# Attention before two expert layers: the masks of the scores, the 1e-9 of the softmax, the warm-up and the table of places

## The chip, the cores and the metric

The kernel runs on one core of a Trainium2 chip. The metric is the device time of one execution in microseconds, as the median of several runs. One execution was also recorded by the profiler; all rows of a trace are from that one.

## What is computed

```python
def reference(**kw):
    x = attention(kw["q"], kw["k"], kw["v"])        # each (2, 12, 448, 64)
    x = x.transpose(0, 2, 1, 3).reshape(896, 768)
    x = moe(x, w_gate, w_val, w_out)                # 768 -> 1536 -> 768
    return moe2(x, w_in, w2_out)                    # 768 -> 2048 -> 768

def attention(q, k, v):                             # causal
    scores = (q @ k.T) / sqrt(64);  scores[above the diagonal] = -1e9
    attn = exp(scores - max(scores))
    return attn / (sum(attn) + 1e-9) @ v

def moe(x, w_gate, w_val, w_out):  return (sigmoid(x @ w_gate) * (x @ w_val)) @ w_out
def moe2(x, w_in, w2_out):
    h = x @ w_in;  return (h * clip(h + 3, 0, 6) / 6) @ w2_out
```

q, k and v are float32; the five weight matrices are float64 and come as 64-bit words.

## The kernel before

**Products.** Every product of two float32 matrices is done as three matmuls in the fp32r form: both operands are split into a rounded part (hi) and the rest (lo), and hi·hi, hi·lo and lo·hi are added in PSUM (`TERMS`).

**Weights.** The weights come in units of 128 partitions by 768 words. A unit is decoded to float32 by ScalarE (L115, scale by the upper words) and VectorE (L120 shift, L124 clamp, L128 join, L134 sign) and then split (hi on ScalarE L153, lo on VectorE L158, or by an accumulating DMA L144). Most of the span is the two expert layers, in which TensorE multiplies and ScalarE and VectorE decode the units to come. The first three units (0, 1 and 2) are decoded within the attention stage, in steps W (load), Wa (L115), Wb (L120), Wc (L124), Wd (L128), We (L134), Wf (hi) and Wg (lo) with the unit's number behind.

**Attention** takes the first 120 us. There are 24 heads, done as 12 pairs. One pair goes through these steps, each named by a letter:

- Lq, Lk, Lv: loads. Tq, Tk: TensorE transposes q and k (four matmuls each). Thq, Thk: ScalarE writes the rounded parts qh and kh (L286). Tlq, Tlk: VectorE writes the rests ql and kl (L293). Vh, Vl: GpSimd splits v.
- S0, S1: scores. The 448 rows of a head are four tiles of queries, tile 0 of 64 rows and tiles 1 to 3 of 128 rows, with 64, 192, 320 and 448 keys. `STILES = [(1, 2), (0, 3)]`: S0 makes tiles 1 and 2, S1 tiles 0 and 3, each in a PSUM buffer of its own (two buffers, `ps_a`). For each tile there are six products (three terms by the two heads of the pair, which use 64 rows of the array each), and then the mask of the diagonal block is added by four more matmuls (two for tile 0) of a bf16 identity by a bf16 mask.
- M0..M3: VectorE takes the negated maximum of a row. E0..E3: ScalarE's exponential with the sum of a row, two instructions a tile, then a third that adds 1e-9 to the two sums. R0..R3: VectorE's reciprocal. N0..N3: GpSimd multiplies the exponentials by it, two instructions a tile.
- C0..C3: TensorE transposes the normalised tiles in four groups; H and J (L377, L383) split them into pth and ptl. D0..D3: the products with the padded v into `pav`. Xh, Xl: ScalarE and VectorE write the attention's output x in two parts (L407, L410).
- F00..F05, F10..F15: the first twelve steps of the expert layer, three matmuls each, with units 0 and 1 and the first batch's x (L190). They run between the steps of the last pairs.
- Z: matmuls of a zeroed tile `idle` by itself, 512 columns each, whose result nobody reads (22 of them).

**The order** of all this is written out by hand. Each step has a place in time: a number from `AT` plus pair × `PERIOD` plus the pair's entry of `SHIFT`, or an absolute number from `OWN` (weights and F) or `WARM` (Z). `when` moves a place behind all that the step needs, and `rings` does so for buffers:

```python
        at = OWN[name] if name in OWN else p * PERIOD + SHIFT[p] + AT[name]
        place[key] = max([at] + [when(a) + 1 for a in need[key]])
for key in sorted(left, key=lambda key: (when(key), key)):
    _, fn, args = left[key]
    fn(*args)
```

So each engine gets its instructions in the order of the places, and then executes them in that order, waiting for what they need.

Of the kernel before, what the change touches and what calls it, by code (L numbers as in the profile page):

```python
# [8 lines left out]
F32 = mybir.dt.float32  # L9
F32R = mybir.dt.float32r  # L10
BF16 = mybir.dt.bfloat16
# [20 lines left out]
def kernel(  # L32
# [178 lines left out]
    with tc.manual_schedule():  # L211

        with ExitStack() as actx:
# [85 lines left out]
            def s_pe(p, ts):  # L299
                both = ps_a.tile([P, 2, 512], F32, tag="m", name="s")  # L300
                off = 0
                for t in ts:
                    rows, n = Q1[t] - Q0[t], Q1[t]
                    ps = both[:, :, off : off + n]
                    off += n
                    for i, (a, c) in enumerate(TERMS):
                        for j in range(2):
                            r = slice(j * D, (j + 1) * D)
                            nc.tensor.matmul(  # L309
                                ps[:, j],  # L310
                                lhsT=live["q" + "hl"[a], p][r, Q0[t] : Q0[t] + P],
                                rhs=live["k" + "hl"[c], p][r, :n],
                                start=(i == 0),
                                stop=(i == 2),
                            )

                    for h in range(rows // D):
                        for j in range(2):
# [6 lines left out]
                    live["s", p, t] = ps[:rows]  # L325

            def column(tag, t):
                return p_sm.tile([P, 2], F32, tag=tag, name=tag)[: Q1[t] - Q0[t]]

            def s_max(p, t):  # L330
                nm = column("nm", t)
                nc.vector.tensor_reduce(nm, live["s", p, t], axis=AX.X, op=ALU.max, negate=True)  # L332
                live["nm", p, t] = nm

            def s_exp(p, t):
                ps, nm, sm = live.pop(("s", p, t)), live.pop(("nm", p, t)), column("sm", t)
                pr = p_p.tile([P, Q1[t] // D, 2, D], F32, tag=f"pr{t}", name="pr")[: Q1[t] - Q0[t]]
                for j in range(2):
# [3 lines left out]
                    )  # L342
                nc.scalar.activation(sm, sm, AF.Copy, bias=1e-9)
                live["pr", p, t], live["sm", p, t] = pr, sm

            def s_rcp(p, t):
                sm, rc = live.pop(("sm", p, t)), column("rc", t)
                nc.vector.reciprocal(rc, sm)  # L348
                live["rc", p, t] = rc

            def s_nrm(p, t):
                pr, rc = live["pr", p, t], live.pop(("rc", p, t))
# [911 lines left out]
```

## Time and profile before

| | |
|---|---|
| Times of three runs | 601.07, 597.39, 599.21 us (median 599.21) |
| The profiled execution | 598.94 us, of which its span is 597.0 |
| Mean granted TensorE clock | 1.000 |
| Busy: TensorE matmuls (PE), weight loads (PEld) | 585.6 us (98%), 536.0 (90%) |
| Busy: VectorE (DVE), ScalarE (ACT), GpSimd (POOL) | 477.0 (80%), 345.2 (58%), 136.6 (23%) |
| Chain that ended last, by engine | DVE 38%, PE 38%, ACT 18%, issue 5% |

The span runs from the first to the last instruction; the 1.9 us beside it lie outside. The busy times are shares of the whole span, and attention is its first fifth, so what a change in attention is worth can't be read from them. The chain is the work that ended last, followed backward from the last instruction through whatever released it. PE is the matmul side of TensorE; PEld is its weight load, which runs beside the matmuls.

### The profile page before, as it was taken

Reading aid. Unit: us, or ns where it says so; the run is one execution under the profiler, and the core shown is the slowest. Engines: PE = TensorE matmul, PEld = TensorE weight load, DVE = VectorE, ACT = ScalarE, POOL = GpSimd, SP = SyncE. Lnnn points to the kernel's source line nnn. Section 1 sums busy time; section 2 is a strip of 40 time slices with the busy share of each in tenths; the row PEclk is TensorE's granted clock in tenths of the full one; section 3 lists DMA queues with packets and bytes.
Section 4 is the critical chain, followed back from the end, with each engine's and each line's share of the span. In section 5 each row is a group of like instructions: output and inputs, shape, how many; then the busy total and the mean of one; then the engine's idle time right before and its main releaser. Section 6 shows DMA issues by size and latency. Waiting matters only on the chain.

```text
span 597.0 us, 9165 instructions
## 1 busy us (share of the span) xinstructions
PE 585.6 (98%) x3436; PEld 536.0 (90%) x3436; DVE 477.0 (80%) x733; ACT 345.2 (58%) x680; POOL 136.6 (23%) x201
## 2 busy tenths in 40 slices
PE   9999999999999999999999999999999999999997
PEld 5887888999998999898999999988998899999997
DVE  6899988578798898899867788888999988867601
ACT  4998999445665666658343332486777555433200
POOL 2988998601111111110000000012222000000000
PEclk9999999999999999999999999999999999999999
DMA  7664314047986767673344433467978424437002
GB/s 174 158 147 109 86 32 122 2 132 184 264 187 173 208 161 182 171 181 110 99 135 159 143 122 107 111 158 172 245 192 207 133 57 133 128 105 246 7 0 93
DMA packets 86684, 82.64 MB, mean 138 GB/s; under 512 B 35312, under 2 KB 77040, under 8 KB 86640
## 3 DMA queue, kind: packets, MB, share of 16 engines
q1 hardware_dynamic: 80448, 64.50, 36.3%
q0 software_dynamic: 6192, 17.57, 16.0%
q8 instruction: 27, 0.44, 0.3%
q14 instruction: 17, 0.14, 0.1%
HBM read 61.73 MB, written 2.75 MB: 108 GB/s over the span
## 4 chain that ended last, share of the span: by engine, by line
DVE 38%; PE 38%; ACT 18%; issue 5%; DMA 1%; SPq 0%; ACTq 0%; DVEq 0%; POOLq 0%
PE w L744 14%; PE m L1197 12%; DVE b L128 7%; DVE b L134 6%; PE pav L394 4%; DVE lo L158 4%; DVE b L124 4%; ACT hi L153 3%; ACT pr L339 3%; ACT b L115 3%; PE pt L367 2%; DVE g L1165 2%; DVE raw L120 2%; PE s L309 2%; DVE g L182 2%
## 5 line engine op out<-in xcount | busy, mean ns | idle before, releaser
L1197 PE MATMUL m<-hi,g 128*128 128x384 f32 x448 | 114.0, 335 | 0.6 <-DVE g L1165 0.6
L153 ACT CAST hi<-b 128x768 fp32r<-128x768 f32 x35 | 29.0, 835 | 105.6 <-DVE b L134 101.3
L1197 PEld LDWEIGHTS m<-hi,g 128*128 128x128 f32 x448 | 80.8, 188 | 1.2 <-DVE g L1165 1.2
L1197 PE MATMUL m<-lo,g 128*128 128x384 f32 x224 | 75.0, 335 | 0.4 <-DVE lo L158 0.4
L744 PE MATMUL w<-T,hi 128*128 128x448 f32 x252 | 71.9, 367 | 1.4 <-ACT g2r L761 1.4
L190 PE MATMUL m<-g,hi 128*128 128x448 f32 x288 | 70.1, 365 | 0.0
L128 DVE SCALAR_TENSOR_TENSOR b<-b,raw 128x768 int32<-128x768 int32 x68 | 67.0, 985 | 2.2
L134 DVE SCALAR_TENSOR_TENSOR b<-raw,b 128x768 int32<-128x768 int32 x68 | 66.2, 974 | 2.3
L115 ACT ACTIVATE b<-raw 128x768 f32<-128x768 f32 x68 | 61.2, 904 | 0.0
L190 PEld LDWEIGHTS m<-g,hi 128*128 128x128 f32 x288 | 54.1, 188 | 4.3
L124 DVE TENSOR_SCALAR b<-b 128x768 f32<-128x768 f32 x68 | 38.5, 566 | 23.4 <-ACT b L115 23.0
L158 DVE TENSOR_TENSOR lo<-b,hi 128x768 fp32r<-128x768 f32 x35 | 33.4, 958 | 28.1 <-ACT hi L153 28.0
L144 POOL DMA_DIRECT2D lo<-S x26 | 25.2, 971 | 130.9 <-ACT lo L143 110.7
L744 PEld LDWEIGHTS w<-T,hi 128*128 128x128 f32 x252 | 46.9, 188 | 6.0 <-ACT g2r L761 2.1
L354 POOL TENSOR_SCALAR pr<-pr,rc 128x320 f32<-128x320 f32 (+3 forms) x96 | 45.4, 489 | 16.7 <-DVE rc L348 14.3
L190 PE MATMUL m<-x,hi 128*128 128x448 f32 x192 | 48.9, 367 | 0.0
L744 PE MATMUL w<-T,lo 128*128 128x448 f32 x126 | 46.3, 367 | 0.9 <-DMA lo<-raw 0.6
L339 ACT ACTIVATE pr<-s,nm 128x192 f32<-128x192 f32 (+3 forms) x96 | 44.4, 470 | 2.6 <-DVE nm L332 1.6
L1197 PEld LDWEIGHTS m<-lo,g 128*128 128x128 f32 x224 | 42.0, 188 | 0.7 <-DVE lo L158 0.7
L394 PE MATMUL pav<-pth,vpad 128*128 128x448 f32 (+6 forms) x168 | 41.2, 311 | 0.1
L190 PE MATMUL m<-g,lo 128*128 128x448 f32 x144 | 40.9, 366 | 0.0
L190 PEld LDWEIGHTS m<-x,hi 128*128 128x128 f32 x192 | 35.9, 188 | 2.8
(140 smaller groups left out, 1249.4 us busy)
## 6 DMA issues: line engine op xcount, KB each, us to landing
raw<-in_moe_w_out_dram SPq DMA_DIRECT2D x28, 768.0 KB, 4.4
raw<-in_moe_w_in_dram SPq DMA_DIRECT2D x16, 768.0 KB, 4.7
lo<-S POOLq DMA_DIRECT2D x26, 384.0 KB, 4.3
raw<-in_moe_w_gate_dram SPq DMA_DIRECT2D x12, 768.0 KB, 5.0
raw<-in_moe_w_val_dram SPq DMA_DIRECT2D x12, 768.0 KB, 5.1
q<-in_q_dram SPq DMA_DIRECT2D x24, 112.0 KB, 2.9
k<-in_k_dram SPq DMA_DIRECT2D x24, 112.0 KB, 3.2
v<-in_v_dram SPq DMA_DIRECT2D x24, 112.0 KB, 2.8
```

The source lines that it names most:

```text
L115: nc.scalar.activation(b, words(u)[0].bitcast(F32), AF.Copy, scale=REBIAS)
L124: nc.vector.tensor_scalar(b, b, UPPER_MAX, -UPPER_MAX, op0=ALU.min, op1=ALU.max)
L128: nc.vector.scalar_tensor_tensor(bi, bi, 3, words(u)[1], op0=ALU.logical_shift_left, op1=ALU.bitwise_or)
L134: nc.vector.scalar_tensor_tensor(bi, words(u)[0], -(2 ** 31), bi, op0=ALU.bitwise_and, op1=ALU.bitwise_or)
L153: nc.scalar.copy(hi, part_t[u])
L158: nc.vector.tensor_sub(lo, part_t.pop(u), split_t[u][0].bitcast(F32))
L190: nc.tensor.matmul(ps[:, b, :S], lhsT=w[a][:, i * P : (i + 1) * P], rhs=x(c, k0 + i, b), start=(first and i == 0 and n == 0), stop=(last a ...
L339: nc.scalar.activation(pr[:, :, j], ps[:, j].rearrange("p (c d) -> p c d", d=D), AF.Exp, bias=nm[:, j : j + 1], accum_out=sm[:, j : j + 1],)
L354: nc.gpsimd.tensor_scalar(pr[:, :, j], pr[:, :, j], rc[:, j : j + 1], 1.0, op0=ALU.mult, op1=ALU.mult)
L394: nc.tensor.matmul(live["pav", p][:, c * D :], lhsT=vpad[p % NV][a][:, c], rhs=pt[e][:, off : off + S - c * D], start=(c == 0 and m == 0), ...
L744: nc.tensor.matmul(ps, lhsT=w[a][:, k * P : (k + 1) * P], rhs=x[:, c, i], start=(first and i == 0 and n == 0), stop=(i == HK - 1 and n == ...
L1197: nc.tensor.matmul(po[t], lhsT=g2[2 * s + i][a][:, t * P : (t + 1) * P], rhs=w[e][:, i * HC : (i + 1) * HC], start=(s == 0 and i == 0 and ...
```

## The change

It has five parts.

- The masks of both tiles of a score block are written into PSUM first (L310), and the six products of each tile are added on top of them (L319).
- The 1e-9 is added once for two tiles, by a step Q0 or Q1 (L350, 128x4) that waits for both tiles' exponentials, and one reciprocal (R0, R1) serves both tiles. The small tiles of sums and the exponentials of tile 0 have 128 rows now, where 64 are used.
- The Z matmuls read a constant bf16 1.0 from the kernel's table of constants. The tile `idle` and the VectorE instruction that zeroed it are gone. There are 30 of them.
- One more of the six tiles of padded v is zeroed by GpSimd, one fewer by VectorE.
- The table of places (`PERIOD`, `SHIFT`, `AT`, `OWN`, `WARM`) has new numbers.

```diff
+                for t in ts:
+                    live["s", p, t] = both[:, :, off : off + Q1[t]]
+                    off += Q1[t]
+                for t in ts:
+                    ps, rows = live["s", p, t], Q1[t] - Q0[t]
                     for h in range(rows // D):
                         for j in range(2):
                             r, c = slice(j * D, (j + 1) * D), (j != h) * D
                             nc.tensor.matmul(
                                 ps[:, j, Q0[t] + h * D :], lhsT=identb[r, c : c + P],
                                 rhs=maskb[r, j * D : (j - h) * D + rows],
+                                start=(t == ts[0] and h == 0), stop=True, skip_group_check=True,
+                            )
+                for t in ts:
+                    for i, (a, c) in enumerate(TERMS):
+                        for j in range(2):
+                            r = slice(j * D, (j + 1) * D)
+                            nc.tensor.matmul(
+                                live["s", p, t][:, j],
+                                lhsT=live["q" + "hl"[a], p][r, Q0[t] : Q0[t] + P],
+                                rhs=live["k" + "hl"[c], p][r, : Q1[t]],
                                 start=False, stop=True, skip_group_check=True,
                             )
...
+            def s_eps(p, g):
+                sm = live["sm", p, g]
                 nc.scalar.activation(sm, sm, AF.Copy, bias=1e-9)
-                live["pr", p, t], live["sm", p, t] = pr, sm
-
-            def s_rcp(p, t):
-                sm, rc = live.pop(("sm", p, t)), column("rc", t)
+
+            def s_rcp(p, g):
+                sm, rc = live.pop(("sm", p, g)), column("rc")
                 nc.vector.reciprocal(rc, sm)
-                live["rc", p, t] = rc
+                for i, t in enumerate(STILES[g]):
+                    live["rc", p, t] = rc[:, i]
...
-            PERIOD = 33902
+            PERIOD = 42229
...
-                "W0": 105210, "W1": 183238, "W2": 259736, "Wa0": 105211, "Wa1": 183239, "Wa2": 259737,
+                "W0": 54321, "W1": 156548, "W2": 758554, "Wa0": 54322, "Wa1": 156549, "Wa2": 758555,
...
-                    add(f"R{t}", [f"E{t}"], s_rcp, t)
-                    add(f"N{t}", [f"R{t}"], s_nrm, t)
+                for i, ts in enumerate(STILES):
+                    add(f"Q{i}", [f"E{t}" for t in ts], s_eps, i)
+                    add(f"R{i}", [f"Q{i}"], s_rcp, i)
+                    for t in ts:
+                        add(f"N{t}", [f"R{i}"], s_nrm, t)
...
-                nc.tensor.matmul(idle_ps, lhsT=idle[:, :P], rhs=idle, start=True, stop=True)
+                nc.tensor.matmul(idle_ps, lhsT=ones[:, :P], rhs=ones, start=True, stop=True)
...
-            idle = const.tile([P, 512], BF16, name="idle")
-            nc.vector.memset(idle, 0.0)
+            ones = nc.const_aps.tensor(1.0, [P, 512], BF16)
...
-                    eng = nc.gpsimd if 2 * i + x < 3 else nc.vector
+                    eng = nc.gpsimd if 2 * i + x < 4 else nc.vector
```

What the table does to the order is shown at three places. A row below is an instruction (line, operation, out<-in, shape of the output), and x2 says how many stand in a row.

TensorE, the second score block S1 of a pair in the middle of attention, before (`s` are the scores, kh, kl, qh, ql the parts of k and q, `pav` the products with v):

```order
L394 MATMUL pav<-pth,vpad_1_109 128x448
L309 MATMUL s<-kh,qh 128x64 x2
L309 MATMUL s<-kl,qh 128x64 x2
L309 MATMUL s<-kh,ql 128x64 x2
L320 LDWEIGHTS identb
L320 MATMUL s<-maskb,identb 128x64
L320 LDWEIGHTS identb
L320 MATMUL s<-maskb,identb 128x64
L309 MATMUL s<-kh,qh 128x448 x2
L309 MATMUL s<-kl,qh 128x448 x2
L309 MATMUL s<-kh,ql 128x448 x2
```

and after:

```order
L310 LDWEIGHTS identb
L310 MATMUL s<-maskb,identb 128x64
L319 MATMUL s<-kh,qh 128x64 x2
L319 MATMUL s<-kl,qh 128x64 x2
L319 MATMUL s<-kh,ql 128x64 x2
L319 MATMUL s<-kh,qh 128x448 x2
L319 MATMUL s<-kl,qh 128x448 x2
L319 MATMUL s<-kh,ql 128x448 x2
L402 MATMUL pav<-pth,vpad_0_108 128x448
```

The block's products now stand in one row, and what follows the block follows a product of 448 columns, not a mask.

ScalarE, the first two pairs' start, before (L339 the exponentials, L343 the added 1e-9, L286 the rounded parts of q and k):

```order
L286 ACTIVATE kh<-tr 128x448
L339 ACTIVATE pr,sm<-s,nm 128x3x64 x2
L343 ACTIVATE sm<-sm 128x2
L339 ACTIVATE pr,sm<-s,nm 128x5x64 x2
L343 ACTIVATE sm<-sm 128x2
L286 ACTIVATE qh<-tr 128x448
L339 ACTIVATE pr,sm<-s,nm 64x64 x2
L343 ACTIVATE sm<-sm 64x2
L339 ACTIVATE pr,sm<-s,nm 128x7x64 x2
L343 ACTIVATE sm<-sm 128x2
```

and after (L342 the exponentials, L350 the added 1e-9):

```order
L286 ACTIVATE kh<-tr 128x448
L342 ACTIVATE pr,sm<-s,nm 128x3x64 x2
L286 ACTIVATE qh<-tr 128x448
L342 ACTIVATE pr,sm<-s,nm 128x5x64 x2
L286 ACTIVATE kh<-tr 128x448
L350 ACTIVATE sm<-sm 128x4
L342 ACTIVATE pr,sm<-s,nm 128x64 x2
L342 ACTIVATE pr,sm<-s,nm 128x7x64 x2
```

The rounded parts of the second pair's q and k moved between the first pair's exponentials, and the first sum leaves ScalarE behind two tiles and both of them.

VectorE, the end of attention, before (L383 the rests of the transposed tiles, L410 the lo part of x, and the decoding of unit 2 and of unit 3):

```order
L128 SCALAR_TENSOR_TENSOR b<-b,raw 128x768
L410 TENSOR_TENSOR x_73<-pav,x_73 128x448
L383 TENSOR_TENSOR ptl<-pt,pth 128x448
L383 TENSOR_TENSOR ptl<-pt,pth 128x512 x2
L383 TENSOR_TENSOR ptl<-pt,pth 128x320
L410 TENSOR_TENSOR x_73<-pav,x_73 128x448
L134 SCALAR_TENSOR_TENSOR b<-raw,b 128x768
L158 TENSOR_TENSOR lo<-b,hi 128x768
L120 TENSOR_SCALAR raw<-raw 128x768
L124 TENSOR_SCALAR b<-b 128x768
```

and after (L391 and L418 are the former L383 and L410):

```order
L391 TENSOR_TENSOR ptl<-pt,pth 128x320
L418 TENSOR_TENSOR x_73<-pav,x_73 128x448
L120 TENSOR_SCALAR raw<-raw 128x768
L124 TENSOR_SCALAR b<-b 128x768
L128 SCALAR_TENSOR_TENSOR b<-b,raw 128x768
L134 SCALAR_TENSOR_TENSOR b<-raw,b 128x768
L158 TENSOR_TENSOR lo<-b,hi 128x768
```

Unit 2's shift, clamp and join (L120, L124, L128) moved behind the last part of x. Elsewhere on TensorE, ten Z now stand ahead of the first transposes (before: six), seven between them and the first score product (before: six), and a third row of transposes (the second pair's q) stands between the first pair's S0 and S1. At the end 27 of the 36 matmuls F stand ahead of the last product with v, where 24 did.

## Rows read from the trace of the kernel before

**Rows 1.** windows: stretch, length, busy PE, PEld, DVE, ACT, POOL, PEclk, DMA

```profile
60.00:98.00 38.00, 38.00 (x369) 33.25 (x366) 33.31 (x73) 35.37 (x127) 34.26 (x54) 1.00 0.36 92
...
120.00:180.00 60.00, 60.00 (x298) 55.62 (x297) 49.92 (x58) 35.14 (x42) 9.60 (x10) 1.00 0.77 194
```

**Rows 2.** timeline of PE, first 16 us: start, length, what, idle before

```profile
1.19 2.74 PE L486 MATMUL pt<-idle 128*128 128x512 bf16 x6 [1.19 <-DVE idle L571]
4.13 0.98 PE L277 MATMUL tr<-identf,q 112*128 112x112 f32 x4 [0.21 <-DMA q<-in_q_dram]
...
5.89 2.77 PE L486 MATMUL pt<-idle 128*128 128x512 bf16 x6
...
9.33 0.45 PE L309 MATMUL s<-kh,qh 64*128 64x192 f32 x2
...
13.09 1.24 PE L486 MATMUL pt<-idle 128*128 128x512 bf16 x5
```

**Rows 3.** chain that ended last, 0 to 130 us: start, length, what

```profile
12.10 0.92 ACT pr L339 x4
...
13.24 1.02 ACT pr L339 x4
...
14.49 0.43 ACT qh L286
...
112.27 3.65 PE m L190 x18
```

**Rows 4.** timeline of POOL from 10 us

```profile
14.89 3.85 POOL L354 TENSOR_SCALAR pr<-pr,rc 128x320 f32<-128x320 f32 x8 [10.00 <-DVE rc L348]
...
22.45 3.64 POOL L354 TENSOR_SCALAR pr<-pr,rc 128x320 f32<-128x320 f32 x8
```

**Rows 5.** timeline of PE from 90.2 us: one score block

```profile
90.30 0.36 PE L309 MATMUL s<-kh,qh 64*128 64x192 f32 x2
90.49 0.27 PE L309 MATMUL s<-kl,qh 64*128 64x192 f32 x2
...
90.72 0.26 PE L320 MATMUL s<-maskb,identb 64*128 64x128 bf16 x4
90.81 0.39 PE L309 MATMUL s<-kh,qh 64*128 64x320 f32 x2
91.04 0.31 PE L309 MATMUL s<-kl,qh 64*128 64x320 f32 x2
...
91.34 0.26 PE L320 MATMUL s<-maskb,identb 64*128 64x128 bf16 x4
91.53 0.60 PE L277 MATMUL tr<-identf,k 112*128 112x112 f32 x4
```

**Rows 6.** timeline of PE: the first score product of four pairs

```profile
45.73 0.36 PE L309 MATMUL s<-kh,qh 64*128 64x192 f32 x2
...
55.74 0.35 PE L309 MATMUL s<-kh,qh 64*128 64x192 f32 x2
...
64.76 0.36 PE L309 MATMUL s<-kh,qh 64*128 64x192 f32 x2
...
81.83 0.36 PE L309 MATMUL s<-kh,qh 64*128 64x192 f32 x2
```

**Rows 7.** chain that ended last, from 119 us

```profile
119.68 0.54 ACT x L407
...
120.87 0.88 DVE b L134
...
123.60 0.47 DVE raw L120
124.07 0.48 DVE b L124
124.57 0.97 DVE b L128
```

**Rows 8.** groups by line and shape, first 120 us: count, busy, mean ns

```profile
L343 ACT ACTIVATE sm<-sm 128x2 f32<-128x2 f32 x36 | 7.3, 204 | 1.1
```

More of the change, by code (lines that the diff above doesn't have):

```diff
@@ L302, in s_pe @@
                 for t in ts:
[L303 to L315, printed above, removed]
+                    live["s", p, t] = both[:, :, off : off + Q1[t]]
+                    off += Q1[t]
+                for t in ts:
+                    ps, rows = live["s", p, t], Q1[t] - Q0[t]
                     for h in range(rows // D):
@@ L322, in s_pe, with column @@
                                 rhs=maskb[r, j * D : (j - h) * D + rows],
+                                start=(t == ts[0] and h == 0), stop=True, skip_group_check=True,
[8 more added lines that the diff above has]
+                                rhs=live["k" + "hl"[c], p][r, : Q1[t]],
                                 start=False, stop=True, skip_group_check=True,
                             )
-                    live["s", p, t] = ps[:rows]
-            def column(tag, t):
-                return p_sm.tile([P, 2], F32, tag=tag, name=tag)[: Q1[t] - Q0[t]]
+            def column(tag):
+                return p_sm.tile([P, 2, 2], F32, tag=tag, name=tag)
             def s_max(p, t):
-                nm = column("nm", t)
+                nm = column("nm")[:, 0]
                 nc.vector.tensor_reduce(nm, live["s", p, t], axis=AX.X, op=ALU.max, negate=True)
@@ L335, in s_exp @@
             def s_exp(p, t):
-                ps, nm, sm = live.pop(("s", p, t)), live.pop(("nm", p, t)), column("sm", t)
-                pr = p_p.tile([P, Q1[t] // D, 2, D], F32, tag=f"pr{t}", name="pr")[: Q1[t] - Q0[t]]
+                g = [t in ts for ts in STILES].index(True)
+                if ("sm", p, g) not in live:
+                    live["sm", p, g] = column("sm")
+                ps, nm = live.pop(("s", p, t)), live.pop(("nm", p, t))
+                sm = live["sm", p, g][:, STILES[g].index(t)]
+                pr = p_p.tile([P, Q1[t] // D, 2, D], F32, tag=f"pr{t}", name="pr")
                 for j in range(2):
@@ L342, in s_exp @@
                     )
+                live["pr", p, t] = pr
+            def s_eps(p, g):
+                sm = live["sm", p, g]
                 nc.scalar.activation(sm, sm, AF.Copy, bias=1e-9)
[L344 to L347 removed]
+            def s_rcp(p, g):
+                sm, rc = live.pop(("sm", p, g)), column("rc")
                 nc.vector.reciprocal(rc, sm)
[L349 removed]
+                for i, t in enumerate(STILES[g]):
+                    live["rc", p, t] = rc[:, i]
             def s_nrm(p, t):
[L352 removed]
+                rows = Q1[t] - Q0[t]
+                pr, rc = live["pr", p, t][:rows], live.pop(("rc", p, t))[:rows]
                 for j in range(2):
@@ L368, in c_pe @@
                                 ps[:, o : o + rows],
-                                live["pr", p, t][:, c].rearrange("p j d -> p (j d)"),
+                                live["pr", p, t][:rows, c].rearrange("p j d -> p (j d)"),
                                 identf[:rows, r : r + rows],
```

5 lines of the change are left out of this document (1 added, 4 removed), and 25 rows, old and new, of tables (AT, OWN, WARM).

## The prediction

> **What bounds the kernel now.** I read the table of stretches first. From 60 to 98 us TensorE (PE) is busy for all of its 38.00 us, VectorE and GpSimd for 35.37 and 34.26, and the clock is full; from 120 to 180 us PE is busy for all 60 as well, VectorE for 49.92 [rows 1]. So in the middle of attention the end is set by what PE has to do, with VectorE and GpSimd close behind, and time is won there only by giving PE less to do. Two places in attention are different, and I read each by itself.
>
> The first is the beginning. The chain that ended last does not run through PE's queue there but through the first pair: from 12.10 to 15 us it is ScalarE's exponentials [rows 3]. PE's own start is a row of idle matmuls at half the speed of later ones: six in the 2.56 us from 5.89 to the next work, 0.427 each, where five from 13.09 take 1.22, 0.244 each [rows 2]. By their spacing these are the lower and the upper of the clock's two levels (1.2 and 2.4 GHz), although the granted clock's mean over the span reads 1.000; for the first 9 us I go by the spacing.
>
> The second is the end. At 119.68 ScalarE begins the last x, and from there the chain goes on as a row of decoding on VectorE and ScalarE, sign first (L134 at 120.87), then the next unit's shift, clamp and join [rows 7]. That row goes on, without a step on PE, until about 250 us. So what stands at its head is worth its whole length, and what PE saves at the end is worth something only if the last x comes earlier.
>
> **The change part by part.** All terms are added to the profiled execution's 598.94 us, which is within 0.27 of the median 599.21.
>
> *a. Start.* The first idle matmul had waited 1.19 us for VectorE's zeroing of its tile [rows 2]. With a constant that wait goes; some 0.8 us of start stays, my estimate from that row, since PE's program still has to begin. Then come ten idle matmuls instead of six, two sets of transposes (1.76 us from 4.13 to 5.89), and seven more idle ones. If all run at the lower level, S0 of the first pair begins at 0.8 + 10 × 0.427 + 1.76 + 7 × 0.427 = 9.8 us, against 9.33 [rows 2]. If the longer run brings the upper level from the transposes on, these take 0.9 us and the seven take 1.71, and S0 begins at some 7.7 to 8.2 with the wait for the load of k. The products of that S0 also run at either level. In all the first exponential moves by between +0.3 and −1.3 us; I take −0.8, nearer to the faster end, since the run of work ahead of the transposes has no gap now. The Trainium skill ("TensorE: Matmul & The Clock Gate", Part 1: The HAM clock gate, What's actually happening) says that the throttled level is the default and that activity releases it; the trace agrees, with 0.427 us in the first 9 us and 0.244 us at 13 us.
>
> *b. From there to the first normalised tile.* Before, GpSimd began at 14.89, some 2.8 us behind the first exponential, with the sums of tile 1 and a qh of 0.43 in between [rows 3, 4]. Now two tiles' exponentials (0.92 and 1.02, [rows 3]), the second pair's qh and kh and one added 1e-9 lie ahead of the reciprocal. Against before that is one kh more in the way (0.43) and the wait for the second tile, less one 1e-9 of 0.204 [rows 8]: +0.6 for GpSimd's first work. Together with a: −0.2, bounds −0.7 and +0.9.
>
> *c. The first pair's S1* has the second pair's q ahead of it on PE (four transposes, 0.5 us at the upper level), and the idle matmuls behind it are fewer by about as much. Nothing.
>
> *d. Masks first.* One S0 takes 1.23 us from 90.30 to 91.53 [rows 5]. Its steps: the first two products 0.19, the next two pairs some 0.115 each, four masks 0.09, then the first two products of the wider tile 0.23 against 0.15 for its later ones, then four masks that need 0.19 until the next work begins. So three places cost more than their work: 0.075 at entry, 0.08 where products follow masks, 0.10 behind the last masks. With masks first, the block has one return from masks to products (0.08 stays) and leaves by a product of 320 columns, behind which a weight load has room (0.10 goes). At the entry I count nothing: a mask with its load takes 0.09 / 4 = 0.022 us in these rows, so an exposed load of it can't be worth more. That is 0.17 for an S0. S1, with the same steps and a tile of half as many masks, comes to 0.14. Nine pairs run in the stretch where PE never waits, from about 30 us on: 9 × 0.31 = −2.8 us. The bounds are 0 (the gaps stay, whichever comes first) and −4.0 (all three gaps go: 0.255 and 0.19 less the price of the masks' entry, by nine).
>
> *e. PE's stalls near 46 and 57 us.* Four starts of S0, at 45.73, 55.74, 64.76 and 81.83 [rows 6], against 8.47 us for a pair where nothing waits (81.83 to 90.30): the first two intervals are 10.01 and 9.02, that is 1.54 and 0.55 too long. There VectorE's ql stands behind two full-size steps of a unit's decoding. The new places spread units 0 and 1 otherwise, and unit 2 is out of the way. I take 1.4 of the 2.1 us as saved and 0.7 as kept; bounds 0 and −2.1.
>
> *f. The end of PE's row.* Three more F matmuls stand ahead of the last product with v. At 3.65 / 18 = 0.203 each [rows 3] that is +0.6 on the last x.
>
> *g. Unit 2's decoding.* Before, only its sign and its split stood behind the last x. Now shift, clamp and join stand there too, at the head of the chain: 0.47 + 0.48 + 0.97 by the same lines for the next unit [rows 7] = +1.9. ScalarE's scale runs beside the shift. PE, which before had no wait in this part, has its work of F and of units 0 and 1 as a buffer, and the chain's later waits (near 187 and 250 us) get longer by the same. Bounds 1.0, if the join hides behind ScalarE's x and scale, and 2.0.
>
> *At nothing:* on ScalarE the two fewer 1e-9 a pair (2 × 0.204 us, [rows 8]) and on VectorE the two fewer reciprocals, because in the dense stretch PE is later than both. What covers them is PE's 8.47 us a pair; were ScalarE the bound, they would be worth 0.4 a pair. Tile 0 on 128 rows has the same number of columns per partition. The zeroing that moves to GpSimd is done before its first tile at 14.89.
>
> Sum: −0.2 + 0 − 2.8 − 1.4 + 0.6 + 1.9 = −1.9, so **597.0 us**.
>
> **The rivals.**
>
> *R1, the masks save nothing.* The 0.255 us in the block may be the price of changing between full-height and half-height matmuls, and of products behind a bf16 load, which come as often as before if the entry is now a mask. For it: the entry alone costs 0.075 today [rows 5]. Against it: the 0.10 behind the last masks is behind matmuls too short to cover a load, and these move. Then the sum is −0.2 − 1.4 + 0.6 + 1.9 = +0.9, or 599.8 us. The Trainium skill ("TensorEngine Tiling (Array Packing)", Tiling Modes, Key Properties) says that changing the tiling mode drains TensorE; by that rule the drain is paid once on entering and once on leaving a block, whatever is first in it. The rows show a price at both ends, but not how much of it is a drain and how much a load.
>
> *R2, GpSimd becomes the bound: slower.* Its eight normalisations take 3.85 us for a first group and it begins the next pair at 22.45, 7.56 us later [rows 4]; it is busy for 34.26 of 38 us [rows 1]. With one reciprocal for two tiles it can start a pair's second half only when ScalarE has done both exponentials of that half: some 3.4 us after the first half's release (two tiles, 1.94, a qh or kh of 0.43, a split of 0.86, the 1e-9), while the first half keeps it for 1.9. If nothing else of its own fills the 1.5 us, a cycle becomes 7.56 + 1.5 = 9.1 us, 0.6 more than PE's 8.47, and nine pairs cost 5.4; PE's stalls vanish in that (−2.1). The sum is 598.94 − 0.2 + 5.4 − 2.1 + 0.6 + 1.9 = 604.5. It decides from the point at which a pair's first normalisation waits for R0 and not for GpSimd's previous work. Against it: GpSimd has a backlog from the first pairs on, so releases that come 1.5 us later find it still at work.
>
> *R3, faster.* The chain behind attention has slack that the profile does not show, because what PE needs first are units 0 and 1, and unit 2 only after their products; then g is 0 and f too, and d reaches its far end: 598.94 − 0.7 − 4.0 − 1.4 = 592.8, about 592.7. For it: PE works without a wait from 120 to 180 us. Against it: the chain that ended last goes through VectorE there.
>
> **How the numbers follow.** Chances: the forecast 0.45, R1 0.25, R3 0.18, R2 0.12. The forecast's own range, with the bounds of a, d, e and g, is about 594 to 600.5. To hold 8 in 10 the range takes in R1, most of R3 and the near part of R2: 592.5 to 602.5. One per cent, 6 us, is about what a measurement of this kernel can tell from no change. Faster by more than that, below 593.2, needs most of R3 and a little of the forecast's tail: 0.14. Slower, above 605.2, is the far half of R2 and a rest for an order that waits somewhere I don't see: 0.09. Within 1%: 0.77.
>
> **What the profile after would show.** a: the first product of S0 before 9 us and the first exponential before 12. b: GpSimd's first normalisation between 14.2 and 15.8. d: S0's first masks to the next work in about 1.06 us, and 8.16 from S0 to S0 in the dense part; R1 would show 1.2 and 8.47. e: intervals of S0 between 30 and 65 us all below 9.3. g: L120, L124 and L128 of unit 2 behind L418, with the chain through them. R2 would show GpSimd idle between the two halves of a pair and intervals of 9 us; R3 no waits of PE near 187 and 250 us. What would make me wrong by more than the range is a clock that falls during attention, or a wait of PE for a step that the new places put late in every pair.

## The result, and the profile after

The changed kernel takes **603.98 us** (median of 5 runs, 603.72 to 604.95) against 599.11 before: a ratio of 1.0088, 95% interval 1.0062 to 1.0114. It is slower by some 5 us, and outside the forecast range. Its profiled execution is the one of 603.98 us, with a span of 602.2.

The first rows are ScalarE's timeline in the first pairs of the changed kernel (start, length, what, and in brackets the idle time ahead and what ended it):

```profile
10.67 0.42 ACT L342 ACTIVATE pr<-s,nm 128x192 f32<-128x192 f32 x1 [3.52 <-DVE nm L331]
...
11.47 0.54 ACT L286 ACTIVATE qh<-tr 128x448 fp32r<-128x448 f32 x1
...
13.37 0.54 ACT L286 ACTIVATE kh<-tr 128x448 fp32r<-128x448 f32 x1 [0.33 <-PE tr L277]
13.81 0.20 ACT L350 ACTIVATE sm<-sm 128x4 f32<-128x4 f32 x1
...
18.45 0.42 ACT L342 ACTIVATE pr<-s,nm 128x192 f32<-128x192 f32 x1 [1.95 <-DVE nm L331]
...
19.26 0.54 ACT L286 ACTIVATE kh<-tr 128x448 fp32r<-128x448 f32 x1
```

The first exponential starts at 10.67 and not at 12.10 [rows 3]. But qh and kh of the next pair stand between the exponentials, and kh at 19.26 could not run before an exponential that had waited 1.95 us for its maximum. What waited for this kh, on VectorE and then on TensorE:

```profile
19.84 0.62 DVE L293 SCALAR_TENSOR_TENSOR kl<-tr,kh 128x448 fp32r<-128x448 f32 x1 [1.47 <-ACT kh L286]
...
20.52 0.60 PE L277 MATMUL tr<-identf,q 112*128 112x112 f32 x4 [0.47 <-DVE kl L293]
```

GpSimd's timeline, to be read against [rows 4]:

```profile
14.86 3.65 POOL L362 TENSOR_SCALAR pr<-pr,rc 128x192 f32<-128x192 f32 x8 [8.87 <-DVE rc L354]
...
23.05 3.65 POOL L362 TENSOR_SCALAR pr<-pr,rc 128x192 f32<-128x192 f32 x8 [0.93 <-DVE rc L354]
...
33.73 1.83 POOL L362 TENSOR_SCALAR pr<-pr,rc 64x64 f32<-64x64 f32 x4 [1.46 <-DVE rc L354]
```

Its first work starts where it did (14.86, before 14.89), its second 0.60 us later. Between the two halves of the third pair it stands idle for 1.46 us, the sign that R2 named, and the chain that ended last runs through it from 23 to 36 us. On TensorE, the first masks of S0 of the first four pairs, then of two pairs in the dense stretch with what follows the last one:

```profile
8.03 0.34 PE L310 MATMUL s<-maskb,identb 64*128 64x128 bf16 x8
...
15.16 0.34 PE L310 MATMUL s<-maskb,identb 64*128 64x128 bf16 x8
...
21.05 0.34 PE L310 MATMUL s<-maskb,identb 64*128 64x128 bf16 x8
...
30.46 0.34 PE L310 MATMUL s<-maskb,identb 64*128 64x128 bf16 x8
...
81.18 0.34 PE L310 MATMUL s<-maskb,identb 64*128 64x128 bf16 x8
...
89.62 0.34 PE L310 MATMUL s<-maskb,identb 64*128 64x128 bf16 x8
...
90.36 0.31 PE L319 MATMUL s<-kl,qh 64*128 64x320 f32 x2
90.50 0.31 PE L319 MATMUL s<-kh,ql 64*128 64x320 f32 x2
90.74 0.39 PE L402 MATMUL pav<-pth,vpad 128*128 128x256 f32 x1
...
91.90 1.04 PE L375 MATMUL pt<-identf,pr 128*128 128x128 f32 x8
92.87 0.29 PE L310 MATMUL s<-maskb,identb 64*128 64x64 bf16 x6
```

The same places in the kernel before (the second and the fourth S0, and the transposes of C with the product D behind them):

```profile
14.31 0.36 PE L309 MATMUL s<-kh,qh 64*128 64x192 f32 x2
...
28.58 0.36 PE L309 MATMUL s<-kh,qh 64*128 64x192 f32 x2
...
91.97 1.04 PE L367 MATMUL pt<-identf,pr 128*128 128x128 f32 x8
92.76 0.45 PE L394 MATMUL pav<-pth,vpad 128*128 128x448 f32 x1
```

The first S0 is 1.3 us earlier than before, the second 0.85 later (15.16 against 14.31), the fourth 1.88 later (30.46 against 28.58). A dense pair takes 8.44 us (81.18 to 89.62), before 8.47 [rows 5, 6]. S0 itself takes 1.12 us (89.62 to 90.74), before 1.23 [rows 5]; but the transposes of C ahead of S1 now need 0.97 until S1 starts, where they took 0.80 with a product D behind them.

At the end of attention TensorE waits once more, at 106.59, for VectorE, which had run a full-size step of unit 1's decoding (L158, 1.57 us) in the row of the last score blocks:

```profile
106.59 1.15 PE L375 MATMUL pt<-identf,pr 128*128 128x128 f32 x8 [0.59 <-DVE ptl L391]
```

Then the chain that ended last, which starts with the last x:

```profile
121.02 0.54 ACT x L415
...
121.58 0.62 DVE x L418
122.21 0.47 DVE raw L120
122.68 0.48 DVE b L124
...
123.18 0.97 DVE b L128
...
124.17 0.97 DVE b L134
...
164.61 5.92 DMA lo<-b
...
170.57 6.75 PE m L190 x32
```

The last x starts at 121.02, 1.34 us later than before; the sign (L134) of unit 2 at 124.17, 3.30 later than its 120.87 [rows 7], since shift, clamp and join stand ahead of it. The chain ends in an accumulating transfer, for which TensorE waits 2.24 us:

```profile
170.57 0.67 PE L190 MATMUL m<-x,lo 128*128 128x448 f32 x2 [2.24 <-DMA lo<-b]
```

The stretch from 120 to 180 us (columns as in [rows 1]) has TensorE busy for 57.17 of 60 us, where before it was busy for all; the other 0.59 is a wait for an earlier transfer of the same kind, at 160.76:

```profile
60.00:98.00 38.00, 38.00 (x371) 32.85 (x369) 33.17 (x63) 34.44 (x117) 33.51 (x54) 1.00 0.39 105
120.00:180.00 60.00, 57.17 (x286) 52.41 (x285) 48.84 (x57) 34.25 (x41) 9.62 (x10) 1.00 0.73 181
```

In the kernel before, the same matmul (the 32nd ahead of the next layer's first) had almost waited too. Its transfer, its weight load and the matmul itself:

```profile
161.18 0.83 POOL L144 DMA_DIRECT2D lo<-b  x1 [6.79 <-ACT lo L143]
lo<-b POOLq DMA_DIRECT2D x1, 384.0 KB, 5.1
...
166.38 0.39 PEld L190 LDWEIGHTS m<-x,lo 128*128 128x128 f32 x2
...
166.58 0.57 PE L190 MATMUL m<-x,lo 128*128 128x448 f32 x2
```

The transfer was issued at 161.18 and landed 5.1 us later, at 166.3: 0.1 us ahead of the weight load that uses it first, 0.3 ahead of the matmul. So TensorE had 0.1 to 0.3 us to spare, which no busy share shows. From there the delay against before goes on as follows. This matmul is 4.0 us later. Behind a second wait (1.46 us at 193.78, before 0.62 at 188.84) it is 4.9. A wait of 0.37 us at 251 is gone, and the delay is 4.2 at 278 us. Behind a new wait of 0.69 us at 424.33 it is 5.2, which is that of the span.

### The profile page after: what moved, and what is told of

The parts are those of the page before. It is cut to its first block, busy times and chain, and to the rows that moved or that the text cites. A ratio compares the mean times of both kernels' runs of the same rounds, so it can differ in the third digit from the quotient of the medians.

```text
span 602.2 us, 9125 instructions
## 1 busy us (share of the span) xinstructions
PE 585.8 (97%) x3443; PEld 534.7 (89%) x3444; DVE 472.1 (78%) x706; ACT 341.7 (57%) x656; POOL 135.3 (22%) x203
## 4 chain that ended last, share of the span: by engine, by line
PE 50%; DVE 30%; ACT 10%; issue 4%; DMA 3%; POOL 2%; ACTq 0%; POOLq 0%; DVEq 0%
PE w L754 23%; PE m L1207 12%; DVE b L128 5%; PE pav L402 5%; DVE b L134 5%; DVE lo L158 4%; PE pt L375 3%; ACT hi L153 3%; DVE b L124 3%; PE s L319 2%; DVE g L1175 2%; DVE raw L120 2%; PE m L190 2%; DVE g L182 2%; DMA g<-b 1%
## 5 line engine op out<-in xcount | busy, mean ns | idle before, releaser
L134 DVE SCALAR_TENSOR_TENSOR b<-raw,b 128x768 int32<-128x768 int32 x68 | 65.4, 962 | 2.3
L128 DVE SCALAR_TENSOR_TENSOR b<-b,raw 128x768 int32<-128x768 int32 x68 | 65.4, 962 | 2.3
L124 DVE TENSOR_SCALAR b<-b 128x768 f32<-128x768 f32 x68 | 39.1, 576 | 24.6 <-ACT b L115 24.3
L158 DVE TENSOR_TENSOR lo<-b,hi 128x768 fp32r<-128x768 f32 x35 | 34.5, 990 | 28.2 <-ACT hi L153 28.1
L362 POOL TENSOR_SCALAR pr<-pr,rc 128x192 f32<-128x192 f32 (+3 forms) x96 | 47.5, 514 | 15.8 <-DVE rc L354 14.7
L342 ACT ACTIVATE pr<-s,nm 128x192 f32<-128x192 f32 (+3 forms) x96 | 45.3, 486 | 8.7 <-DVE nm L331 7.3
```

The source lines that it names most:

```text
L124: nc.vector.tensor_scalar(b, b, UPPER_MAX, -UPPER_MAX, op0=ALU.min, op1=ALU.max)
L128: nc.vector.scalar_tensor_tensor(bi, bi, 3, words(u)[1], op0=ALU.logical_shift_left, op1=ALU.bitwise_or)
L134: nc.vector.scalar_tensor_tensor(bi, words(u)[0], -(2 ** 31), bi, op0=ALU.bitwise_and, op1=ALU.bitwise_or)
L158: nc.vector.tensor_sub(lo, part_t.pop(u), split_t[u][0].bitcast(F32))
L342: nc.scalar.activation(pr[:, :, j], ps[:, j].rearrange("p (c d) -> p c d", d=D), AF.Exp, bias=nm[:, j : j + 1], accum_out=sm[:, j : j + 1],)
L362: nc.gpsimd.tensor_scalar(pr[:, :, j], pr[:, :, j], rc[:, j : j + 1], 1.0, op0=ALU.mult, op1=ALU.mult)
```

## The experiments

Every run was timed in 5 rounds beside the kernel before on the same chip; the ratio is to that. "Last x" is the start of ScalarE's last x in its profile, "E to x" the time to it from the first exponential, since the start itself varies (below). In the diffs of the table of places a line shows only the entries that change, and entries of several lines can stand in one.

| run | median us | ratio to before (95%) | first exponential | last x | E to x |
|---|---|---|---|---|---|
| before | 598.2 to 599.1 | 1 | 12.10 | 119.68 | 107.58 |
| changed | 603.98 | 1.0088 (1.0062 to 1.0114) | 10.67 | 121.02 | 110.35 |
| b_masks_first | 597.88 | 0.9998 (0.9984 to 1.0012) | 10.36 | 117.31 | 106.95 |
| b_w2_late | 600.74 | 1.0041 (1.0025 to 1.0058) | 10.17 | 117.77 | 107.60 |
| a_old_table | 597.43 | 0.9987 (0.9977 to 0.9998) | 11.43 | 117.24 | 105.81 |
| a_w2_early | 603.69 | 1.0097 (1.0081 to 1.0112) | 10.60 | 124.03 | 113.43 |
| a_w2_gap | 601.14 | 1.0040 (1.0024 to 1.0055) | 9.96 | 120.29 | 110.33 |
| a_tq_first | 604.16 | 1.0089 (1.0066 to 1.0112) | 10.63 | 120.14 | 109.51 |
| a_kh_first | 602.25 | 1.0054 (1.0038 to 1.0071) | 9.84 | 117.83 | 107.99 |
| a_ramp | 602.12 | 1.0058 (1.0035 to 1.0082) | 10.26 | 118.53 | 108.27 |
| a_d_order | 606.75 | 1.0135 (1.0111 to 1.0159) | 9.86 | 122.64 | 112.78 |
| a_tail | 602.82 | 1.0060 (1.0037 to 1.0083) | 10.03 | 118.95 | 108.92 |
| a_masks_last | 604.76 | 1.0093 (1.0068 to 1.0119) | 9.54 | 120.42 | 110.88 |
| a_all_four | 598.52 | 0.9989 (0.9974 to 1.0005) | 10.48 | 118.48 | 108.00 |
| a_old_w2_done | 596.91 | 0.9969 (0.9955 to 0.9983) | 11.29 | 117.11 | 105.82 |
| a_best | 595.28 | 0.9937 (0.9917 to 0.9957) | 11.95 | 116.86 | 104.91 |

**The code or the table?** The changed kernel with the old numbers, and with the step Q and the steps R and N behind what they need:

```diff
-            PERIOD = 42229
+            PERIOD = 33902
...
+                "N1": 15036, "N2": 2048, "N0": 25765, "N3": 25766, "Q0": 2046, "Q1": 25763, "R0": 2047, "R1": 25764,
```

> The changed kernel's code with the places of the kernel before (the new step Q and the steps R, N put directly behind what they need). Theory now (the new places made attention end 1.3 us later and moved unit 2): as before or up to 1.5 us less, 597.6 to 599.1, with the last product with v ending at or before 119.5. Rival (the code itself is slower: GpSimd waits for one reciprocal per two tiles): 602 or more, with intervals of 9 us between S0 blocks.

It came out at 597.43, ratio 0.9987. With the old places the new code is not slower than the kernel before; attention is 1.8 us shorter than before (E to x 105.81 against 107.58), and a dense pair takes 8.32 us. GpSimd's first work comes 2.58 us behind the first exponential, before 2.79, so the one reciprocal for two tiles costs nothing there. The 5 us are in the table.

**The masks.** In the kernel before:

```diff
+                for t in ts:
+                    ps, rows = live["s", p, t], Q1[t] - Q0[t]
...
+                                start=(t == ts[0] and h == 0), stop=True, skip_group_check=True,
...
+                for t in ts:
+                    for i, (a, c) in enumerate(TERMS):
```

> The kernel before with one edit: the masks of both tiles of a score block first, products on top; table of places as before. My forecast's term d: 2.8 us less than before (599.1 to 596.3). Theory now (the step from full-height to half-height matmuls keeps its price, so a block gives 0.1 us, a pair 0.1 to 0.2): 1 to 1.5 us less, 597.6 to 598.1. Rival R1: no change, 599.1. An S0 block would take 1.06, 1.12 and 1.23 us.

A dense pair took 8.33 us and not 8.47, so 0.14 is saved, half of what I had costed: S0 went from 1.23 to 1.13 and S1 from 1.30 to 1.25. The time did not change, which the expectation above had wrong. Its last x was 2.37 us earlier than in the profile of before (1.74 of it by the start), the wait-prone matmul 1.73 earlier (164.85; its transfer took 6.0 us), the end 0.6. Some 1.7 us of what is lost on the way is the slower of two spacings of TensorE's matmuls (last section), which this trace has from 300 to 390 us and that of before has not. And in the changed kernel the other way round, with the old order within a block (the edit of L303 to L325 taken back):

> The changed kernel with the masks behind the products of each tile, as in the kernel before. Theory (masks first save 0.14 us a pair, in any order of the blocks): a pair 8.55 to 8.6 us in the dense stretch instead of 8.44, the last product with v 1.2 us later, 604.5 to 605.5. Rival (in the new order a block stands behind transposes and the saving is gone there): 8.44, 604.

The dense pair went from 8.44 to 8.55: masks first is worth 0.11 there. E to x rose by 0.53, where 1.2 was expected, and the time, 1.0093, can't be told from the changed kernel's 1.0088. S1 starts 0.97 us behind the transposes of C here too, with a product first and not a mask, so that price does not come from the mask. So the masks save in both orders, and the new order spends it again on C ahead of S1.

**Unit 2 behind the last x.** First in the kernel before:

```diff
-                "W0": 105210, "W1": 183238, "W2": 259736, "Wa0": 105211, "Wa1": 183239, "Wa2": 259737,
+                "W0": 105210, "W1": 183238, "W2": 758554, "Wa0": 105211, "Wa1": 183239, "Wa2": 758555,
...
-                "Wb2": 284401, "Wc2": 259738, "Wd2": 456361, "We2": 536564, "Wf2": 536565, "Wg2": 536566,
+                "Wb2": 758555, "Wc2": 758556, "Wd2": 758557, "We2": 758558, "Wf2": 758559, "Wg2": 758560,
```

> The kernel before with one edit: unit 2's load and decoding at the changed kernel's places, behind the last x; everything else as before. Forecast's term g: +1.9 us (601.0). Theory now (the chain starts 1.9 later, and the units behind it then land after TensorE wants them, with transfers that collide): +1.9 to +3.5, 601 to 602.6, and TensorE waits near 165 to 170 us that before are not there. Rival R3 (slack in the chain): no change, 599.1.

It cost 2.5 us (1.0041). E to x is the same as before (107.60), so unit 2 had cost attention nothing, and TensorE waited 2.98 us at the same matmul:

```profile
167.87 0.93 PE L190 MATMUL m<-x,lo 128*128 128x448 f32 x2 [2.98 <-DMA lo<-b]
```

This wait cost more than its length, which I hadn't expected: the two stretches are the wait and the 3.3 us behind it (last columns: clock, DMA share, GB/s):

```profile
164.60:167.80 3.20, 0.29 (x2) 0.00 (x0) 3.10 (x6) 2.13 (x3) 0.85 (x1) 1.00 0.51 100
167.90:171.20 3.30, 3.30 (x9) 2.91 (x10) 3.27 (x6) 2.63 (x5) 0.56 (x1) 0.53 1.02 265
```

The granted clock was 0.53, the lower level, and matmuls ran every 0.37 us for 0.20: about 1.5 us on top of the wait. (Against the profile of before, 1.93 us of this is covered by the earlier start.)

Moving it back into the changed kernel, at the places that it had, scaled to the new period:

```diff
-                "W2": 758554, "Wa2": 758555, "Wb2": 758555, "Wc2": 758556, "Wd2": 758557,
+                "W2": 294580, "Wa2": 398500, "Wb2": 330000, "Wc2": 398501, "Wd2": 520000,
```

> The changed kernel with one edit: unit 2's load, scale, shift, clamp and join back inside attention. Theory now: 2 to 3.5 us less than the changed kernel's 604.0 (600.5 to 602), with TensorE's waits at 168 and 192 us shorter by as much. Rival (the code of the softmax and the masks costs the time, not the places): 604.

That failed: the clamp stood ahead of VectorE's work for the pair and waited 0.96 us for its scale, which itself had waited 1.53 us on ScalarE for another full-size step of VectorE (L158). TensorE waited 0.71 us at 100.27 and 1.35 at 104.01, and E to x is 3.1 us longer (113.43). What it gained behind attention it had lost in it. So the same with the steps in an idle stretch:

```diff
+                "W2": 330000, "Wa2": 490000, "Wb2": 490000, "Wc2": 490001, "Wd2": 490002,
```

> The changed kernel with unit 2's scale, shift, clamp and join put into the 4 us in which ScalarE and VectorE stand idle near 109 to 113 us (its load earlier too). Theory (the chain behind the last x starts 1.96 us later by unit 2, and TensorE waits for the weights at its end): the last product with v as in the changed kernel, 120.7, the chain 2 us earlier, TensorE's waits at 168 and 192 us shorter by 2 in all; 601.5 to 602.5. Rival (the end hangs on the last product with v alone): 604.

601.14, ratio 1.0040: 2.9 us of the loss are gone, with E to x as in the changed kernel (110.33). The chain shows the sign directly behind x:

```profile
120.29 0.54 ACT x L415
...
120.85 0.62 DVE x L418
121.48 0.88 DVE b L134
```

and the wait is 0.68 us:

```profile
167.43 0.67 PE L190 MATMUL m<-x,lo 128*128 128x448 f32 x2 [0.68 <-DMA lo<-b]
```

**The first pairs.** One step of the second pair first (a line that gives four steps of pair 1 places of their own):

```diff
+            FIRST = {(1, "Lq"): -137745, (1, "Tq"): -137744, (1, "Thq"): -137743, (1, "Tlq"): -137742}
...
+                        at = FIRST.get(key, at)
```

> The changed kernel with one edit: the second pair's q (load, transpose, qh, ql) ahead of the first score block, as in the kernel before. Theory (the ramp of the first pairs is late because the second pair's k waits for this q, all through one PSUM buffer): the second S0 1 to 1.5 us earlier, GpSimd's second start too, the last product with v 1 to 1.5 us earlier, and the time 1 to 1.5 us less, some 602.7. Rival (one reciprocal for two tiles makes GpSimd late, and the ramp follows that): the last product with v as before, 604.

The second S0 came 0.91 us earlier and E to x fell by 0.84, a little less than expected; the time did not fall (1.0089). In its profile TensorE ran at a granted clock of 0.55 behind the wait that begins at 167 us, for 3 us. That run and one more of the six have a mean clock of 0.996; the other four lie between 602.6 and 604.3. Then one number of the table:

```diff
-                "E0": -48833, "E1": -88195, "E2": -72783, "E3": -41061,
+                "E0": -48833, "E1": -72784, "E2": -72783, "E3": -41061,
```

> The changed kernel with one number of the table changed: tile 1's exponentials (E1) directly ahead of tile 2's, so that the next pair's kh stands ahead of both on ScalarE, as in the kernel before, and not between them. Theory (kh waits behind exponentials that wait for their maximum; kl, the transposes in the one PSUM buffer and the next S0 wait for it): the interval from the third to the fourth S0 8.4 to 8.6 us instead of 9.41, the last product with v 0.8 to 1.2 us earlier from the first exponential on, 602.5 to 603.2. Rival (GpSimd, late by the reciprocal for two tiles, sets that interval): 9.4, 604.

602.25, ratio 1.0054: 2 us better than the changed kernel, and E to x fell by 2.36, more than twice what I had expected. The interval from the third to the fourth S0 is 8.69 and not 9.41, and the two before it are shorter by 0.95 and 0.69. Its S0 started at

```profile
13.45 0.34 PE L310 MATMUL s<-maskb,identb 64*128 64x128 bf16 x8
...
18.65 0.34 PE L310 MATMUL s<-maskb,identb 64*128 64x128 bf16 x8
...
27.34 0.34 PE L310 MATMUL s<-maskb,identb 64*128 64x128 bf16 x8
```

where the changed kernel has 15.16, 21.05 and 30.46; ScalarE's kh runs ahead of both exponentials:

```profile
16.13 0.54 ACT L286 ACTIVATE kh<-tr 128x448 fp32r<-128x448 f32 x1 [1.35 <-PE tr L277]
16.67 0.42 ACT L342 ACTIVATE pr<-s,nm 128x192 f32<-128x192 f32 x1
...
22.79 0.56 ACT L286 ACTIVATE kh<-tr 128x448 fp32r<-128x448 f32 x1
23.59 0.42 ACT L342 ACTIVATE pr<-s,nm 128x192 f32<-128x192 f32 x1 [0.24 <-DVE nm L331]
```

Both edits together:

> Both ramp edits at once: a_kh_first and a_tq_first. Theory: their gains add, the last product with v 1.7 to 2.1 us earlier from the first exponential on (110.1 down to 108.2), 601.5 to 602.5. Rival (the two remove the same wait): as the better one alone.

They do not add (E to x 108.27, ratio 1.0058): the two remove the same wait, the rival's case.

**The products D.** The old order of D0 to D3 around the score blocks:

```diff
-                "D0": 38645, "D1": 55320, "D2": 55321, "D3": 64991, "Xh": 64992, "Xl": 64993,
+                "D0": 25000, "D1": 38645, "D2": 55321, "D3": 55322, "Xh": 55323, "Xl": 55324,
```

> The changed kernel with the products D of a pair in the old order: D0 ahead of S1, D1 behind it, D2 and D3 ahead of S0, so that no score block stands behind a transpose of C. Theory (the price of entering a half-height block depends on the work ahead of it: 0.17 us behind a transpose, nothing behind a product with v): a pair takes 8.32 us in the dense stretch instead of 8.44, the last product with v comes 1 us earlier, 603. Rival (the masks themselves save only 0.03 us a pair): 8.44 and 604.

A miss. Two pairs took 8.33 and 8.32 us, as the theory has it, but others 8.4 to 9.0: the steps on the other engines, which kept their places, seem to come late for them, which is not shown; the last x was 1.6 us later and the time 606.75. The two short pairs agree with a price of 0.12 us a pair (8.44 to 8.32) for the order with S1 behind C; that it can be saved in this table is not shown.

**The tail.**

```diff
-                "F00": 496558, "F01": 496559, "F02": 496560, "F03": 727169,
+                "F00": 496558, "F01": 496559, "F02": 496560, "F03": 496561,
...
-                "Wf1": 460184, "Wg1": 460185,
+                "Wf1": 490000, "Wg1": 490001,
```

with F04 and F05 behind F03, two of the second unit's products at 549121, the rest behind attention.

> The changed kernel with its tail as in the kernel before: 24 and not 27 F matmuls ahead of the last product with v, and unit 1's two parts (L153, L158) out of the row of the last score blocks into the 4 us in which ScalarE and VectorE stand idle. Theory (0.6 us by term f, 0.66 by TensorE's wait at 106 behind L158): the last product with v 1.2 us earlier, time 1 to 1.5 us less than the changed kernel, some 602.7. Rival (the tail's work only changes places with the work behind it): 604.

E to x fell by 1.43, the ratio to 1.0060 (602.82). In the profile the wait at 106.59 and the three F matmuls together were on the way to the last x; the two are not told apart, and the ratio's interval overlaps that of the changed kernel.

**Four at once.** a_tq_first, a_tail, a_w2_gap, and unit 2's sign and parts at 540000 to 540002:

> The changed kernel with four of its placements undone at once: the second pair's q first (a_tq_first), the tail (a_tail), unit 2's scale to join in the first idle stretch (a_w2_gap), and its sign and parts in the second one. Masks, the step Q, warm-up and the rest of the table as in the changed kernel. Theory (these placements and the decoding chain hold the whole loss): last product with v near 118.5 us, no wait of TensorE at 168 us, 597 to 599. Rival (half of the loss sits elsewhere, in the masks or in the reciprocal for two tiles): 600.5 or more.

598.52, ratio 0.9989: 5.9 us less than the changed kernel, so these placements hold the whole loss, with masks first, the step Q and the warm-up left as they are. Some of it is more than an undoing: the sign and the parts stand ahead of the last x in neither kernel, and are worth some 1.1 us in the next run (about as much as the intervals there allow to be told from nothing). GpSimd's idle time between the halves of the third pair is the same 1.46 us here, so it did not hold the loss.

**A faster version.** Since the chain behind the last x decides, the rest of unit 2 was moved ahead of it, with the old table:

```diff
-                "We2": 536564, "Wf2": 536565, "Wg2": 536566,
+                "We2": 470000, "Wf2": 470001, "Wg2": 470002,
```

> The changed kernel's code with the old places (run a_old_table), and unit 2's sign and its two parts moved into the 3.5 us in which VectorE stands idle near 111 to 114 us. Theory (what TensorE waits for near 164 and 187 us is the chain of decoding that starts with the last x): the chain 2.8 us earlier, no wait at 164, 1 to 1.6 us less than a_old_table, some 596. Rival (the wait is for the loads or the accumulating transfer, whenever the decoding is done): as a_old_table, 597.4.

596.91, ratio 0.9969, with no wait near 164 us. Then VectorE's double steps ahead of ql, behind the stalls of [rows 6]:

```diff
-                "We0": 152501, "We1": 221304, "Wf0": 186674, "Wg0": 186675,
+                "We0": 176000, "We1": 251000, "Wf0": 194500, "Wg0": 194501,
```

> Run a_old_w2_done with three more moves on VectorE: the sign of units 0 and 1 half a pair behind their join, and unit 0's parts behind the next pair's ql, so that no ql of q waits for two full-size steps. Theory (these waits cost the pairs at 44 and 53 us 0.9 each): intervals of S0 of 8.4 instead of 9.2 and 9.3, the last product with v 1 to 1.5 us earlier, time 0.5 to 1.5 less than a_old_w2_done, some 596. Rival (TensorE then waits for weights behind attention): as a_old_w2_done.

595.28, ratio 0.9937 (0.9917 to 0.9957): 3.8 us faster than before and 9 faster than the changed kernel. E to x fell by another 0.91, though one interval of 9.14 is left at 62 us, so the stalls are not all gone.

## Why the prediction was wrong

I forecast 597.0 (no change that can be told), and it is slower by 5. Two terms of the sum failed by 2.6 us each: **c**, "nothing" for what follows the first pair, and **d**, whose −2.8 came to −0.2. A third was missing: what a later chain of decoding costs beyond its own length, 1.9 us, was not in the sum. Against the profile of before, the last x is 1.34 us later, where the sum had it 3.8 earlier, made up so:

- **a and b** together −0.03, forecast −0.2. Each was larger than I had it: the first exponential −1.43, the way from there to the first normalised tile +1.40 (2.79 to 4.19). That they cancel is luck. Ten traces with the new places have the first exponential at 9.54 to 10.67 (mean 10.2), six with the old ones at 10.17 to 12.10 (mean 11.2). So the new start is worth about 1 us in the mean, and the profile of before is the latest of all; no run changes the warm-up alone. The first ten Z stand 0.42 us apart and the seven behind the transposes 0.23, as the faster case of a has it. The granted clock reads 1.00 from 0.5 to 9 us in both kernels, so the lower level there rests on the spacing alone. Of b's +1.40, 0.9 goes with kh: in a_kh_first that way is 3.30 (9.84 to 13.14).
- **c** +2.6, forecast 0: 1.9 from the first normalised tile to the fourth pair's S0, and 0.7 in the interval behind it. That interval takes 8.46 us like the later ones, but holds 15 products with v where they hold 21; the six (a D3, which stands behind S0 from there on) are still to be done at the end. I followed the first pair to GpSimd, found that it comes out even, and took the rest as even. But kh of the next pair stands behind an exponential that waits for its maximum, kl waits for kh, the one PSUM buffer of the transposes for kl, and the next pair's scores for that. The order rows of ScalarE show this kh between the exponentials, and I costed it at its own 0.43 us. a_kh_first moves it and gets 2.4 us back; its interval with 15 products still takes 8.43.
- **d** −0.2, forecast −2.8. Masks first does save, 0.14 us a pair in the old order (8.47 to 8.33) and 0.11 in the new one (8.55 to 8.44), half of the 0.31. What I had wrong is the step "0.10 goes" behind the block: the last products of S0 need 0.24 us until the next work (90.50 to 90.74), the ones before them 0.14 (90.36 to 90.50), so a block that ends with a product of 320 columns is left at the same 0.10 as one that ends with masks. And the new order spends most of the rest: C ahead of S1 takes 0.17 more than C ahead of a product D, and I had counted nothing for the entry. So R1 came near in this term, though the masks do save. The Trainium skill ("TensorEngine Tiling (Array Packing)", Tiling Modes, Key Properties) has a drain at each change of mode; the trace agrees in so far as there is a price at both ends of a block, whatever stands first or last in it, but no run here shows how much of it is a drain.
- **e** −2.3, forecast −1.4: four intervals of S0 from 30.46 to 64.30 take 8.46 each, where the same pairs took 36.18 us in all before.
- **f** +0.6 as forecast, and +0.7 for the wait at 106.59, which I had not seen in the order of VectorE; a_tail takes both away and gives 1.43.

**g** was right in mechanism and size on the chain (x to sign 1.19 before, 3.15 after: +1.96), and too small on the time: a_w2_gap gives 2.9 and b_w2_late 2.5. The sum had nothing for what the later chain meets: a transfer of 5.9 us where it took 5.1, and longer or new waits near 193 and 424 us. The trace of before had the number that denies any slack (R3), 0.1 to 0.3 us between a landing and its use, but I read busy shares and waits there, and a wait that just doesn't happen is in neither.

So what I counted as a loss at one end and a gain at the other was a loss at both: last x +1.34 where I had −3.8, chain +1.96, and 1.9 more from transfers and waits behind it.

**R2** gave a time near the measured one (604.5), by luck. Its sign, GpSimd idle between the halves of a pair, shows for 1.46 us in the third pair, but a_all_four has the same and the time of the kernel before; a_old_table has the same reciprocal for two tiles and a shorter attention; and the dense pairs run at 8.44 and not at 9.1 us. **R3** falls by b_w2_late.

Not settled: why a_d_order's pairs differ, how much of a block's two prices is a drain, and what sets the spacing of the matmuls (below), which by itself makes a difference of more than a microsecond between traces. The profiles of before and of the changed kernel both have the quicker spacing from 300 to 390 us, so their 5.2 us don't come from it there.

## What to carry to other kernels

Where an order is written by hand, a step's place is worth what the queue behind it waits for, not its own length: for each step that moves between two others, ask which of them waits, and follow what the moved step releases for two or three rounds, not for one. Behind a stage that ends in a long chain, look for the uses that come just after a landing; a gap of 0.1 to 0.3 us is a bound even where nothing waits. Work at such a chain's head is cheapest in the idle stretches of the same engines just ahead of it; the same work put a few steps earlier, where the engine is full, cost as much as it saved (a_w2_early against a_w2_gap).

## What the runs showed of the hardware

Matmuls of 448 columns in a row stood 202.7 ns apart in some stretches and 206.7 in others, at the same granted clock. The stretch from 300 to 390 us of the kernel before and of a_best, the same code there (busy PE with its count, then PEld and the others; clock before the last two):

```profile
300.00:390.00 90.00, 90.00 (x445) 83.43 (x445) 70.42 (x100) 35.33 (x51) 1.14 (x2) 1.00 0.43 128
```

```profile
300.00:390.00 90.00, 90.00 (x437) 81.74 (x437) 71.72 (x103) 37.29 (x54) 1.70 (x2) 1.00 0.45 132
```

445 against 437 matmuls in 90 us, so some 1.7 us for the same work. Eleven of the sixteen traces were at 206.7 in this stretch, with old and new tables among both kinds. In a_best the slower spacing begins near 290 us with no wait of TensorE beside it. What chooses it stays open.

The transfer that the chain ends in (384 KB, accumulating) took 4.8 to 6.6 us from issue to landing in the sixteen traces; what makes the difference was not tested. And after the waits of 2.98 us (b_w2_late) and 1.76 (a_tq_first) TensorE ran at a granted clock of 0.53 and 0.55 for some 3 us, and after 1.78 us in a_kh_first it fell too (0.50 from 168.9 to 171.0 us). Behind the 2.24 us of the changed kernel's profile and 1.79 us in a_masks_last it stayed at 1.00, so the length of the wait alone doesn't decide.
